# Two heads on the array at once, as row halves for the scores and column halves for the values, with interleaved selection chains and a hand-written TensorE order

## The chip, the cores and the metric

The kernel runs on one core of a Trainium2 chip. The metric is the device time of one execution in microseconds. The core has a matrix engine (TensorE, PE in the profile, with its weight loads as PEld), a vector engine (VectorE, DVE), an activation engine (ScalarE, ACT), GpSimd (POOL) and a queue that issues loads (SyncE, SP). [...]

## The reference

Attention that keeps, in each row, the 32 largest scores, followed by a mixer. All numbers are float32; the mixer's parameters arrive as float64.

```python
# q, k, v: (8 batches, 8 heads, 576 rows, 64)
scores = q @ k.T / sqrt(64)
kth = the 32nd largest score of each row
scores = where(scores >= kth, scores, -1e9)
attn = exp(scores - max)
attn = attn / (sum(attn) + 1e-9)
x = concat over heads of attn @ v          # (8, 576, 512)
# mixer, for each batch: U (576, 32), V (32, 576), w_ch1 (512, 2048), w_ch2 (2048, 512)
u = x + (x.T @ U @ V).T
out = u + maximum(u @ w_ch1, 0) @ w_ch2
```

## The kernel before

Heads go in pairs, four pairs to a batch, 32 in all. `prep` transposes q and k of a pair, so that head 0 has its 64 features on partitions 0 to 63 and head 1 on 64 to 127. The 576 query rows of a head are four chunks of 128 and a tail of 64; the two tails of a pair share one chunk. So a pair has nine score chunks (`CH`), a batch 36, the kernel 288.

For each chunk, `front` does the scores (line 198: two products of 64 features by 288 keys into two banks of PSUM, and ScalarE's copy to `Ssb` on line 205) and then the selection on VectorE. `select` finds the eight largest (`max`, line 215), replaces them by a very small number (`match_replace`, line 222, two instructions in the trace: a short load of the eight values and the replacement), and so on: four times `max`, three times `match_replace`, each on the result of the one before. ScalarE writes exp(score - max) into `E` meanwhile (lines 218 and 219), and line 224 sets to zero what is below the 32nd value.

Four chunks of a head make a `back_head`: `transposed` turns `E` on TensorE so that the keys are on the partitions (line 247; five key chunks, the last of 64 rows; ScalarE copies each to `PT`, line 249), and `values` multiplies: the turned probabilities (128 keys by 128 queries) are the stationary operand, v with a column of ones (65 columns) is streamed (line 255). The 65th column gives the row's sum, and `normalise` divides by it on VectorE (lines 265 to 267) and writes `X`. `back_tail` does the same for the tail chunk.

The mixer of a batch is a generator that yields shares of TensorE's work: U and V (lines 307 and 321), the turning of X (line 334), the first layer (line 345, with ScalarE's relu on line 355) and the second (line 362). `fill` takes pieces of the mixer of the batch before between the score chunks of the present one. The mixer of the last batch runs after all attention. The loop visits the chunks in order; what follows from a chunk comes two chunks later (`LAG`). The framework's planner then orders the instructions of each engine.

In the first 36 chunk steps the mixer's parameters are read and rounded to float32 on VectorE and GpSimd (`f64_round`), one parameter slab a step (`next_param`). SP's queue issues the loads of q, k, v and of the parameters, GpSimd's queue the stores of the output.

PSUM's eight banks: two for the scores (one buffer of two banks), two for transposes, one for `O`, three for the mixer.

Of the kernel before, what the change touches and what calls it, by code (L numbers as in the profile page):

```python
# [15 lines left out]
#: The upper word of 2**-126 as float64, read as float32: smaller magnitudes become 0.  # L16
# [4 lines left out]
def kernel(  # L21
# [33 lines left out]
    NV = 3  # L55

# [12 lines left out]
    vas = [const.tile([P, 2, NT + 1, D + 1], F32, name=f"va{i}") for i in range(NV)]  # L69
    for t in vas:  # L70
        nc.gpsimd.memset(t[:, :, :, D : D + 1], 1.0)
# [12 lines left out]
    def f64_raw(src):  # L84
# [16 lines left out]
        # Sign and top exponent bit stay; of the other ten exponent bits the lower seven.  # L101
# [43 lines left out]
    raw, qkTs, Xs = {}, {}, {}  # L145
    probs = {}

    def load(g):
# [14 lines left out]
        for i in range(2):  # L163
            nc.sync.dma_start(
                va[:, i, 0:NT, 0:D],
                v[b, h0 + i, 0:MAIN, :].rearrange("(p t) d -> p t d", t=NT),
            )
        nc.sync.dma_start(
            va[0:TAIL, :, NT, 0:D], v[b, h0 : h0 + 2, MAIN:S, :].rearrange("h p d -> p h d")
# [3 lines left out]
    def prep(g):  # L173
        """q and k of a pair of heads, transposed: [head and feature, (q | k), row]."""
        tiles = raw.pop(g)
        qkT = attn.tile([P, 2, S], F32, tag="qkT", name="qkT")
        for i, t in enumerate(tiles):
# [12 lines left out]
        qkTs[g] = qkT  # L190

    def scores(g, h, t, Ssb, r0):
        n = rows(t)
        hp = slice(h * D, (h + 1) * D)
        qkT = qkTs[g]
        sc = ps_s.tile([P, 2, 512], F32, tag="sc", name="sc")
        for i in range(2):
            nc.tensor.matmul(  # L198
                sc[0:n, i, 0:HALF],
                lhsT=qkT[hp, 0, cols(t)],  # L200
                rhs=qkT[hp, 1, i * HALF : (i + 1) * HALF],
                start=True,
                stop=True,
            )
        nc.scalar.copy(  # L205
            Ssb[r0 : r0 + n, :].rearrange("p (a n) -> p a n", a=2), sc[0:n, :, 0:HALF]
        )

    def select(Ssb):
        """exp(score - max) where the score is among the row's top TOPK, else 0."""  # L210
        E = attn.tile([P, S], F32, tag="E", name="E", bufs=8)
        cur = Ssb
        for i in range(TOPK // 8):
            m = small.tile([P, 8], F32, tag="m8", name="m8")
            nc.vector.max(m, cur)  # L215
            if i == 0:
                nmax = small.tile([P, 1], F32, tag="nmax", name="nmax", bufs=4)
                nc.scalar.mul(nmax, m[:, 0:1], -SCALE)  # L218
                nc.scalar.activation(E, Ssb, AF.Exp, bias=nmax, scale=SCALE)  # L219
            if i < TOPK // 8 - 1:  # L220
                nxt = attn.tile([P, S], F32, tag="rr", name="rr")
                nc.vector.match_replace(nxt, m, cur, NEG)  # L222
                cur = nxt
        nc.vector.scalar_tensor_tensor(  # L224
            out=E, in0=Ssb, scalar=m[:, 7:8], in1=E, op0=ALU.is_ge, op1=ALU.mult
        )
        return E

    def front(g, i):
        Ssb = attn.tile([P, S], F32, tag="Ssb", name="Ssb", bufs=3)  # L230
        if i < 2 * NT:
            scores(g, i // NT, i % NT, Ssb, 0)
        else:
            for h in range(2):
                scores(g, h, NT, Ssb, h * TAIL)
            del qkTs[g]
        probs[g, i] = select(Ssb)

    def transposed(chunks):
        """The chunks' probabilities with the keys on the partitions, a tile for each key chunk."""  # L240
        width = P * len(chunks)
        PTs = []
        for j in range(NT + 1):
            n = rows(j)
            tp = ps_t.tile([P, 4 * P], F32, tag="tp", name="tp")
            for i, E in enumerate(chunks):
                nc.tensor.transpose(tp[0:n, i * P : (i + 1) * P], E[:, cols(j)], ident)  # L247
            PT = attn.tile([P, 4 * P], F32, tag="PT", name="PT", bufs=6)
            nc.scalar.copy(PT[0:n, 0:width], tp[0:n, 0:width])  # L249
            PTs.append(PT)  # L250
        return PTs

    def values(O, PTs, va, h, c0, n):
        for j in range(NT + 1):
            nc.tensor.matmul(  # L255
                O,
                lhsT=PTs[j][0 : rows(j), c0 : c0 + n],
                rhs=va[0 : rows(j), h, j, :],
                start=(j == 0),
                stop=(j == NT),  # L260
            )

    def normalise(dst, O, n, m):
        den = small.tile([P, NT], F32, tag="den", name="den", bufs=4)
        nc.vector.tensor_scalar_add(den[0:n, 0:m], O[:, :, D], 1e-9)  # L265
        nc.vector.reciprocal(den[0:n, 0:m], den[0:n, 0:m])
        nc.vector.tensor_tensor(  # L267
            dst,
            O[:, :, 0:D],
            den[0:n, 0:m].rearrange("p m -> p m ()").to_broadcast([n, m, D]),  # L270
            ALU.mult,
        )
# [6 lines left out]
    def back_head(g, h):  # L279
# [172 lines left out]
```

## Time and profile before

| what | value |
|---|---|
| time, median of 3 runs | 2581.9 us (2578.86 to 2586.32) |
| span of the profiled execution | 2562.4 us (its own time isn't listed) |
| TensorE busy | 2431.2 us, 95% |
| TensorE's weight loads busy | 1503.1 us, 59% |
| VectorE busy | 1927.5 us, 75% |
| ScalarE busy | 848.4 us, 33% |
| mean granted TensorE clock | 0.888 |

The span runs from the first to the last instruction of the program; the time of a run also holds what lies around it. Matmuls are pipelined, so a busy TensorE isn't one at its peak, and an instruction's recorded duration is longer than the distance to the next one's start. Each fp32 product appears as two matmul instructions with a weight load each; a transpose as one.

### The profile page before, as it was taken

Reading aid. Unit: us, or ns where it says so; the run is one execution under the profiler, and the core shown is the slowest. Engines: PE = TensorE matmul, PEld = TensorE weight load, DVE = VectorE, ACT = ScalarE, POOL = GpSimd, SP = SyncE. Lnnn points to the kernel's source line nnn. Section 1 sums busy time; section 2 is a strip of 40 time slices with the busy share of each in tenths; the row PEclk is TensorE's granted clock in tenths of the full one; section 3 lists DMA queues with packets and bytes.
Section 4 is the critical chain, followed back from the end, with each engine's and each line's share of the span. In section 5 each row is a group of like instructions: output and inputs, shape, how many; then the busy total and the mean of one; then the engine's idle time right before and its main releaser. Section 6 shows DMA issues by size and latency. Waiting matters only on the chain.

```text
span 2562.4 us, 26533 instructions
## 1 busy us (share of the span) xinstructions
PE 2431.2 (95%) x9888; PEld 1503.1 (59%) x9888; DVE 1927.5 (75%) x3716; ACT 848.4 (33%) x1777; POOL 170.1 (7%) x157
## 2 busy tenths in 40 slices
PE   5586599999999999999999999999999999999998
PEld 3354366575656656575565656566565755666555
DVE  7999988877887787778777777877787787778300
ACT  2222233333333333333333334333342433334101
POOL 3445500000000000000000000000000000000000
PEclk9656589998899989999899989999899998999899
DMA  3222200000000000000000000000000000000000
GB/s 90 62 71 75 64 14 5 25 14 23 10 19 21 9 18 15 23 12 23 15 11 19 15 23 12 20 17 16 12 15 23 17 18 14 9 7 5 5 8 11
DMA packets 123202, 56.55 MB, mean 22 GB/s; under 512 B 116480, under 2 KB 116640, under 8 KB 123072
## 3 DMA queue, kind: packets, MB, share of 16 engines
q1 hardware_dynamic: 120128, 45.40, 7.0%
q0 software_dynamic: 2944, 9.44, 1.1%
q8 instruction: 78, 1.28, 0.2%
q14 instruction: 52, 0.43, 0.1%
HBM read 45.38 MB, written 9.44 MB: 21 GB/s over the span
## 4 chain that ended last, share of the span: by engine, by line
PE 89%; DVE 8%; issue 1%; ACT 1%; SPq 0%; DMA 0%; POOL 0%; DVEq 0%; ACTq 0%
PE mm L362 24%; PE mm L345 22%; PE O L255 16%; PE sc L198 14%; PE tp L247 7%; DVE m L215 3%; DVE rr L222 2%; PE mm L307 2%; PE mm L321 2%; PE tp L180 1%; PE tp L334 1%; DVE E L224 1%; DVE bits L105 1%; DVE bits L108 1%; DVE bits L102 0%
## 5 line engine op out<-in xcount | busy, mean ns | idle before, releaser
L215 DVE MAX8 m<-rr 128x8 f32<-128x576 f32 x864 | 654.6, 758 | 19.7
L362 PE MATMUL mm<-w,hT 128*128 128x512 f32 (+1 forms) x1280 | 633.7, 642 | 0.0
L345 PE MATMUL mm<-uT,w 128*128 128x256 f32 (+1 forms) x2048 | 578.0, 435 | 0.7 <-ACT uT L337 0.7
L198 PE MATMUL sc<-qkT 64*128 64x288 f32 (+1 forms) x1280 | 467.5, 479 | 11.8 <-ACT Ssb L205 11.3
L345 PEld LDWEIGHTS mm<-uT,w 128*128 128x128 f32 x2048 | 401.5, 203 | 131.6 <-issue 34.0
L255 PE MATMUL O<-va,PT 128*128 128x65 f32 (+3 forms) x3200 | 468.6, 287 | 0.5 <-DVE X L267 0.4
L255 PEld LDWEIGHTS O<-va,PT 128*128 128x128 f32 (+3 forms) x3200 | 415.3, 195 | 64.1 <-issue 10.4
L222 DVE MATCH_REPLACE8 rr<-m,rr 128x576 f32<-128x576 f32 x576 | 427.1, 741 | 0.0
L362 PEld LDWEIGHTS mm<-w,hT 128*128 128x128 f32 (+1 forms) x1280 | 233.4, 192 | 314.7 <-issue 309.9
L205 ACT COPY Ssb<-sc 128x576 f32<-128x576 f32 (+1 forms) x320 | 203.6, 636 | 511.4 <-PE sc L198 490.8
L215 DVE MAX8 m<-Ssb 128x8 f32<-128x576 f32 x288 | 216.0, 750 | 185.1 <-ACT Ssb L205 183.2
L198 PEld LDWEIGHTS sc<-qkT 64*128 64x128 f32 (+1 forms) x1280 | 215.4, 194 | 213.7 <-issue 108.1
L247 PE MATMUL tp<-ident,E 128*128 128x128 f32 (+1 forms) x1440 | 240.8, 298 | 105.0 <-DVE E L224 104.4
L247 PEld LDWEIGHTS tp<-ident,E 128*128 128x128 f32 (+1 forms) x1440 | 166.5, 143 | 210.0 <-DVE E L224 122.0
L249 ACT COPY PT<-tp 128x512 f32<-128x512 f32 (+3 forms) x480 | 212.0, 480 | 221.8 <-PE tp L247 221.4
L224 DVE SCALAR_TENSOR_TENSOR E<-Ssb,m,E 128x576 f32<-128x576 f32 x288 | 235.7, 818 | 12.1 <-ACT hT L355 0.5
L355 ACT ACTIVATE hT<-mm 128x320 f32<-128x320 f32 (+1 forms) x256 | 104.8, 409 | 421.4 <-PE mm L345 421.2
L219 ACT ACTIVATE E<-Ssb,nmax 128x576 f32<-128x576 f32 x288 | 223.4, 776 | 9.1
L222 DVE MATCH_REPLACE8 rr<-m,Ssb 128x576 f32<-128x576 f32 x288 | 213.6, 742 | 0.0
L218 ACT ACTIVATE nmax<-m 128x1 f32<-128x1 f32 x288 | 58.4, 203 | 367.9 <-DVE m L215 351.2
L265 DVE TENSOR_SCALAR den<-O 128x4 f32<-128x4 f32 (+1 forms) x96 | 14.7, 154 | 204.8 <-PE O L255 204.7
L374 POOL DMA_DIRECT2D out_dram<-ob x32 | 17.7, 555 | 1983.2 <-DVE ob L372 1983.2
(43 smaller groups left out, 786.4 us busy)
## 6 DMA issues: line engine op xcount, KB each, us to landing
raw<-in_moe_w_ch_dram SPq DMA_DIRECT2D x32, 512.0 KB, 3.7
ld_q<-in_q_dram SPq DMA_DIRECT2D x64, 128.0 KB, 2.7
ld_k<-in_k_dram SPq DMA_DIRECT2D x64, 128.0 KB, 2.7
va<-in_v_dram SPq DMA_DIRECT2D x64, 128.0 KB, 2.5
out_dram<-ob POOLq DMA_DIRECT2D x32, 256.0 KB, 2.5
ld_q<-in_q_dram SPq DMA_DIRECT2D x32, 32.0 KB, 2.4
ld_k<-in_k_dram SPq DMA_DIRECT2D x32, 32.0 KB, 2.4
va<-in_v_dram SPq DMA_DIRECT2D x32, 32.0 KB, 2.4
```

What stands on the lines that cost most here:

```text
L198: nc.tensor.matmul(sc[0:n, i, 0:HALF], lhsT=qkT[hp, 0, cols(t)], rhs=qkT[hp, 1, i * HALF : (i + 1) * HALF], start=True, stop=True,)
L205: nc.scalar.copy(Ssb[r0 : r0 + n, :].rearrange("p (a n) -> p a n", a=2), sc[0:n, :, 0:HALF])
L215: nc.vector.max(m, cur)
L219: nc.scalar.activation(E, Ssb, AF.Exp, bias=nmax, scale=SCALE)
L222: nc.vector.match_replace(nxt, m, cur, NEG)
L224: nc.vector.scalar_tensor_tensor(out=E, in0=Ssb, scalar=m[:, 7:8], in1=E, op0=ALU.is_ge, op1=ALU.mult)
L247: nc.tensor.transpose(tp[0:n, i * P : (i + 1) * P], E[:, cols(j)], ident)
L249: nc.scalar.copy(PT[0:n, 0:width], tp[0:n, 0:width])
L255: nc.tensor.matmul(O, lhsT=PTs[j][0 : rows(j), c0 : c0 + n], rhs=va[0 : rows(j), h, j, :], start=(j == 0), stop=(j == NT),)
L345: nc.tensor.matmul(ph[:, 0:width], lhsT=w1[:, cc, f * P : (f + 1) * P], rhs=uT[:, cc, 0:width], start=(cc == 0), stop=(cc == NC - 1),)
L355: nc.scalar.activation(hTs[f][:, 0:width], ph[:, 0:width], AF.Relu)
L362: nc.tensor.matmul(po[0:n, :], lhsT=hTs[f][:, offs[t] : offs[t] + n], rhs=w2[:, f, :], start=(f == 0), stop=(f == NF - 1),)
```

## The change

- A step is now one query chunk of both heads of a pair: five steps to a pair (the fifth is the two tails), 160 steps in all.
- Scores: for each half of the keys, head 0 (rows 0 to 63 of the array) and head 1 (rows 64 to 127) follow each other, into different banks. `ps_s` has two buffers, four banks.
- Selection: the two heads' chains take turns, instruction by instruction. Line 224's successor also writes the row's sum (`accum_out`), and v loses its column of ones.
- Values: v (keys by 64) is the stationary operand, and the turned probabilities (128 queries) are streamed. Head 0 writes partitions 0 to 63 of `O`, head 1 partitions 64 to 127, in turn. The result has the features on the partitions; ScalarE collects it in `XT`, and `to_x` turns it back on TensorE and multiplies by the reciprocal sums on VectorE. The tail's probabilities are divided on GpSimd before they are turned.
- Order: TensorE's instructions stay in the order of the program (`manual_schedule`); the planner orders the other engines. What follows from a step comes one step later. A step calls `fill` eight times, each with an eighth of the step's share of the mixer's two layers; the U and V part and the first turning of X go one piece to a call before that.
- The mixer's banks go from three to two, `O` uses the banks of the transposes. Two parameter slabs are read a step.

```diff
-    ps_s = ctx.enter_context(tc.tile_pool(name="ps_s", bufs=1, space=bass.MemoryType.PSUM))
+    ps_s = ctx.enter_context(tc.tile_pool(name="ps_s", bufs=2, space=bass.MemoryType.PSUM))
     ps_t = ctx.enter_context(tc.tile_pool(name="ps_t", bufs=2, space=bass.MemoryType.PSUM))
-    ps_o = ctx.enter_context(tc.tile_pool(name="ps_o", bufs=1, space=bass.MemoryType.PSUM))
-    ps_m = ctx.enter_context(tc.tile_pool(name="ps_m", bufs=3, space=bass.MemoryType.PSUM))
+    ps_m = ctx.enter_context(tc.tile_pool(name="ps_m", bufs=2, space=bass.MemoryType.PSUM))
+    ctx.enter_context(tc.manual_schedule(engines={PE}))
...
+    def scores(g, t):
+        qkT = qkTs[g]
+        n = rows(t)
+        S2 = attn.tile([P, 2, S], F32, tag="Ssb", name="Ssb", bufs=2)
+        scs = [ps_s.tile([P, 2, 512], F32, tag="sc", name="sc") for _ in range(2)]
+        for i, sc in enumerate(scs):
+            for h in range(2):
+                nc.tensor.matmul(
+                    sc[slice(0, n) if t < NT else half(h), h, 0:HALF],
+                    lhsT=qkT[half(h), 0, cols(t)],
+                    rhs=qkT[half(h), 1, i * HALF : (i + 1) * HALF],
+                    start=True,
+                    stop=True,
+                )
+        for i, sc in enumerate(scs):
+            cs = slice(i * HALF, (i + 1) * HALF)
+            if t < NT:
+                nc.scalar.copy(S2[:, :, cs], sc[:, :, 0:HALF])
...
+    def select(chunks, sums):
+        Es = [attn.tile([P, S], F32, tag="E", name="E", bufs=6) for _ in chunks]
+        curs, ms = list(chunks), [None] * len(chunks)
+        for i in range(TOPK // 8):
+            for c in range(len(chunks)):
+                m = small.tile([P, 8], F32, tag="m8", name="m8")
+                nc.vector.max(m, curs[c])
+                ms[c] = m
+                if i == 0:
+                    nmax = small.tile([P, 1], F32, tag="nmax", name="nmax", bufs=4)
+                    nc.scalar.mul(nmax, m[:, 0:1], -SCALE)
+                    nc.scalar.activation(Es[c], chunks[c], AF.Exp, bias=nmax, scale=SCALE)
+            if i < TOPK // 8 - 1:
+                for c in range(len(chunks)):
+                    nxt = attn.tile([P, S], F32, tag="rr", name="rr", bufs=4)
+                    nc.vector.match_replace(nxt, ms[c], curs[c], NEG)
+                    curs[c] = nxt
+        for c in range(len(chunks)):
+            nc.vector.scalar_tensor_tensor(
+                out=Es[c], in0=chunks[c], scalar=ms[c][:, 7:8], in1=Es[c],
+                op0=ALU.is_ge, op1=ALU.mult, accum_out=sums[c],
             )
...
+            den = small.tile([P, 1], F32, tag="dent", name="dent", bufs=2)
+            (E,) = select(chunks, [den])
+            nc.vector.tensor_scalar_add(den, den, 1e-9)
+            nc.vector.reciprocal(den, den)
+            nc.gpsimd.tensor_scalar(E, E, den, None, ALU.mult)
...
+    def back(g, t):
+        Es, va = probs.pop((g, t)), vas[g % NV]
+        nh = len(Es)
+        PT = attn.tile([P, NT + 1, 2, P], F32, tag="PT", name="PT")
+        per = 4 // nh
+        for j0 in range(0, NT + 1, per):
+            js = range(j0, min(j0 + per, NT + 1))
+            n = rows(js[0])
+            tp = ps_t.tile([P, per, nh, P], F32, tag="tp", name="tp")
+            for j in js:
+                for h, E in enumerate(Es):
+                    nc.tensor.transpose(tp[0 : rows(j), j - j0, h, :], E[:, cols(j)], ident)
+            nc.scalar.copy(PT[0:n, j0 : js[-1] + 1, 0:nh, :], tp[0:n, 0 : len(js)])
+            yield
+        m = rows(t)
+        O = ps_t.tile([P, P], F32, tag="tp", name="O")
+        for j in range(NT + 1):
+            for h in range(2):
+                nc.tensor.matmul(
+                    O[half(h), 0:m],
+                    lhsT=va[0 : rows(j), h, j, :],
+                    rhs=PT[0 : rows(j), j, h, :] if nh == 2 else PT[0 : rows(j), j, 0, half(h)],
+                    start=(j == 0),
+                    stop=(j == NT),
+                )
+        if t == 0:
+            XTs[g] = attn.tile([P, S], F32, tag="XT", name="XT")
+        nc.scalar.copy(XTs[g][:, cols(t)], O[:, 0:m])
+        yield
+
+    def to_x(g):
+        X, XT, den = get_x(g // NPAIR), XTs.pop(g), dens.pop(g)
+        cs = slice((g % NPAIR) * P, (g % NPAIR + 1) * P)
+        nc.vector.tensor_scalar_add(den, den, 1e-9)
+        nc.vector.reciprocal(den, den)
+        tp = ps_t.tile([P, NT, P], F32, tag="tp", name="tp")
         for t in range(NT):
+            nc.tensor.transpose(tp[:, t, :], XT[:, cols(t)], ident)
+        nc.vector.tensor_tensor(
+            X[:, 0:NT, cs].rearrange("p t (h d) -> p t h d", h=2),
+            tp.rearrange("p t (h d) -> p t h d", h=2),
+            den.rearrange("p t h -> p t h ()").to_broadcast([P, NT, 2, D]),
+            ALU.mult,
         )
+        yield
+        tp = ps_t.tile([P, P], F32, tag="tp", name="tp")
+        nc.tensor.transpose(tp[0:TAIL, :], XT[:, cols(NT)], ident)
+        nc.scalar.copy(X[0:TAIL, NT, cs], tp[0:TAIL, :])
+        yield
...
+    MLP_WORK = NF * NC * S / C + NF * (NT + 1) + 1.2
+    CH = NT + 1
+    STEPS = NP * CH
+    PARTS = 8
+    share = MLP_WORK / (NPAIR * CH * PARTS)
...
+    for n in range(STEPS + 1):
+        g, t = divmod(n, CH)
+        gb, tb = divmod(n - 1, CH)
         if g < NP:
+            if t == 0 and g + 1 < NP:
                 load(g + 1)
+            if t == 1:
+                ready = prep(g + 1) if g + 1 < NP else iter(())
+            front(g, t)
         next_param()
+        next_param()
+        fill(3)
+        if n >= 1:
+            for _ in back(gb, tb):
+                fill()
+            if tb == NT:
+                for _ in to_x(gb):
                     pass
+                if (gb + 1) % NPAIR == 0:
+                    mixing = mixed(gb // NPAIR)
+        if g < NP and t >= 1:
+            next(ready, None)
+        fill()
+    for _ in mixing:
         pass
+    for f in fillers:
+        for _ in f:
+            pass
```

## Rows read from the trace of the kernel before

**Rows 1.** Page, busy time of each engine, share and instructions.
```profile
PE 2431.2 (95%) x9888; PEld 1503.1 (59%) x9888; DVE 1927.5 (75%) x3716; ACT 848.4 (33%) x1777; POOL 170.1 (7%) x157
```

**Rows 2.** Windows: from:to, length, busy of PE, PEld, DVE, ACT, POOL; clock; DMA.
```profile
200.00:300.00 100.00, 65.88 (x275) 43.17 (x274) 99.93 (x200) 30.74 (x63) 52.91 (x36) 0.62 0.25 74
...
919.20:1216.20 297.00, 296.50 (x1239) 183.65 (x1237) 231.05 (x443) 105.95 (x222) 2.73 (x5) 0.92 0.07 17
...
1072.10:1075.60 3.50, 3.50 (x6) 1.00 (x6) 3.34 (x9) 0.00 (x0) 0.00 (x0) 0.51 0.00 0
```

**Rows 3.** Timeline of VectorE: start, duration, instruction; last line 224 of batches 0, 7.
```profile
323.25 0.80 DVE L224 SCALAR_TENSOR_TENSOR E<-Ssb,m,E 128x576 f32<-128x576 f32 x1
...
2394.79 0.82 DVE L224 SCALAR_TENSOR_TENSOR E<-Ssb,m,E 128x576 f32<-128x576 f32 x1
```

**Rows 4.** Timeline of TensorE, merged: start, duration, instructions and their count.
```profile
1014.16 3.60 PE L362 MATMUL mm<-w,hT 128*128 128x512 f32 x8
1017.68 1.23 PE L198 MATMUL sc<-qkT 64*128 64x288 f32 x4
1018.85 3.70 PE L362 MATMUL mm<-w,hT 128*128 128x512 f32 x8
1022.48 1.23 PE L198 MATMUL sc<-qkT 64*128 64x288 f32 x4
...
1028.15 0.75 PE L198 MATMUL sc<-qkT 64*128 64x288 f32 x2
1028.83 1.09 PE L247 MATMUL tp<-ident,E 128*128 128x128 f32 x8
```

**Rows 5.** Groups of the period 919.2 to 1216.2: busy, mean ns, idle before.
```profile
L255 PE MATMUL O<-va,PT 128*128 128x65 f32 (+3 forms) x403 | 57.9, 283 | 0.0
L198 PE MATMUL sc<-qkT 64*128 64x288 f32 (+1 forms) x160 | 53.9, 448 | 0.5 <-ACT Ssb L205 0.5
```

**Rows 6.** Timeline of TensorE's matmuls and weight loads in one block of values.
```profile
1066.12 0.62 PE L247 MATMUL tp<-ident,E 128*64 128x128 f32 x4
1066.59 0.56 PE L255 MATMUL O<-va,PT 128*128 128x65 f32 x4
...
1067.66 4.52 PE L255 MATMUL O<-va,PT 64*128 64x65 f32 x32
1072.12 1.11 PE L362 MATMUL mm<-w,hT 128*64 128x512 f32 x1
...
1067.42 4.62 PEld L255 LDWEIGHTS O<-va,PT 64*128 64x128 f32 x32
```

**Rows 7.** Timeline of VectorE inside a period.
```profile
1205.73 0.76 DVE L215 MAX8 m<-rr 128x8 f32<-128x576 f32 x1
...
1207.38 0.76 DVE L215 MAX8 m<-rr 128x8 f32<-128x576 f32 x1
1208.06 0.74 DVE L215 MAX8 m<-Ssb 128x8 f32<-128x576 f32 x1
1208.72 0.80 DVE L224 SCALAR_TENSOR_TENSOR E<-Ssb,m,E 128x576 f32<-128x576 f32 x1
1209.43 0.08 DVE L222 MATCH_VALUE_LOAD rr<-m,Ssb 128x8 f32 x1
1209.51 0.74 DVE L222 MATCH_REPLACE8 rr<-m,Ssb 128x576 f32<-128x576 f32 x1
1210.17 0.68 DVE L372 TENSOR_TENSOR ob<-X,mm 128x512 f32<-128x512 f32 x1
```

**Rows 8.** Groups over the whole span, by shape: a GpSimd product with a scalar.
```profile
L115 POOL TENSOR_SCALAR mask<-mask 128x512 f32<-128x512 f32 x32 | 47.6, 1487 | 13.9 <-DVE mask L113 13.9
```

**Rows 9.** Timeline of TensorE near the end, with what ended its wait.
```profile
2395.59 0.66 PE L247 MATMUL tp<-ident,E 128*128 128x128 f32 x4 [0.24 <-ACT PT L249]
```

**Rows 10.** Waits in the period 919.2 to 1216.2: total us, times, longest.
```profile
DVE m L215 <- ACT Ssb L205: 26.5, 15, 4.0
DVE den L265 <- PE O L255: 26.5, 9, 6.4
```

More of the change, by code (lines that the diff above doesn't have):

```diff
@@ L81, in cols, with half @@
         return slice(t * P, t * P + rows(t))
+    def half(h):
+        return slice(h * D, (h + 1) * D)
     def f64_raw(src):
@@ L209, in select @@
[L209 to L227, printed above, removed]
@@ L253, in values @@
[L253 to L272, printed above, removed]
+        S2 = attn.tile([P, 2, S], F32, tag="Ssb", name="Ssb", bufs=2)
@@ new lines, in scores @@
+        return [S2[:, 0], S2[:, 1]] if t < NT else [S2[:, 0]]
+    def select(chunks, sums):
[17 more added lines that the diff above has]
+            nc.vector.scalar_tensor_tensor(
+                out=Es[c],
+                in0=chunks[c],
+                scalar=ms[c][:, 7:8],
+                in1=Es[c],
+                op0=ALU.is_ge,
+                op1=ALU.mult,
+                accum_out=sums[c],
+            )
+        return Es
@@ new lines, in front @@
+    def front(g, t):
+        if t == 0:
+            dens[g] = small.tile([P, NT, 2], F32, tag="den", name="den", bufs=3)
+        chunks = scores(g, t)
+        if t < NT:
+            probs[g, t] = select(chunks, [dens[g][:, t, h : h + 1] for h in range(2)])
+        else:
+            den = small.tile([P, 1], F32, tag="dent", name="dent", bufs=2)
[3 more added lines that the diff above has]
+            nc.gpsimd.tensor_scalar(E, E, den, None, ALU.mult)
+            probs[g, t] = [E]
+            del qkTs[g]
@@ L315, in mixer @@
         nc.scalar.copy(Tb, pT[0:R, :])
-        yield 5
-        for t in range(NT + 1):
+        yield
+        for t in (0, 1, NT, 2, 3):
             n = rows(t)
@@ L356, in mixer @@
                 yield NC * width / C
-            for t in chunks:
+            for i, t in enumerate(chunks):
                 n = rows(t)
@@ L376, in mixer @@
                     nc.gpsimd.dma_start(out[b, MAIN:S, :], ob[0:n, :])
-                yield 4
-    MIXER_WORK = 5 + (NT + 1) + 0.3 * (NT + 1) + NF * NC * S / C + NF * (NT + 1)
-    CH = 2 * NT + 1
-    LAG = 2
-    per_step = MIXER_WORK / (NPAIR * CH - 1)
-    filler, due = iter(()), 0.0
-    def fill(work):
-        nonlocal due
-        due += work
-        while due > 0:
-            done = next(filler, None)
-            if done is None:
-                due = 0.0
-                break
-            due -= done
+                yield 2
@@ new lines, in mlp, with fill @@
+                if k == 0 and i < 2:
+                    if i == 0:
+                        ahead = turn(b, HALVES[1])
+                    turned = next(ahead)
+                    yield 0.6
+        del Xs[b]
+    MLP_WORK = NF * NC * S / C + NF * (NT + 1) + 1.2
[3 more added lines that the diff above has]
+    share = MLP_WORK / (NPAIR * CH * PARTS)
+    fillers, mixing, due = [], iter(()), 0.0
+    def fill(n=1):
+        nonlocal due
+        for _ in range(n):
+            next(mixing, None)
+            due += share
+            while due > 0:
+                if not fillers:
+                    due = 0.0
+                    break
+                done = next(fillers[0], None)
+                if done is None:
+                    fillers.pop(0)
+                else:
+                    due -= done
@@ L397, with mixed @@
+    def mixed(b):
+        yield
+        yield from mix(b)
+        for first in turn(b, HALVES[0]):
+            yield
+        fillers.append(mlp(b, first))
     load(0)
     next_param()
-    prep(0)
-    for n in range(NP * CH + LAG):
-        g, i = divmod(n, CH)
+    for _ in prep(0):
+        pass
+    for n in range(STEPS + 1):
+        g, t = divmod(n, CH)
+        gb, tb = divmod(n - 1, CH)
         if g < NP:
-            if i == 0 and g + 1 < NP:
+            if t == 0 and g + 1 < NP:
@@ L404 @@
                 load(g + 1)
-            front(g, i)
-            if i == CH - 2 and g + 1 < NP:
-                prep(g + 1)
+            if t == 1:
+                ready = prep(g + 1) if g + 1 < NP else iter(())
+            front(g, t)
         next_param()
-        fill(per_step)
-        gb, ib = divmod(n - LAG, CH)
-        if n >= LAG and ib in (NT - 1, 2 * NT - 1):
-            back_head(gb, ib // NT)
-        elif n >= LAG and ib == CH - 1:
-            back_tail(gb)
-            if (gb + 1) % NPAIR == 0:
-                for _ in filler:
-                    pass
-                filler, due = mixer(gb // NPAIR), 0.0
```

115 lines of the change are left out of this document (38 added, 77 removed).

## Prediction

> **What bounds the kernel now.** I read the totals of the page first, then the stretches, one period in its groups, and last the order of time inside it. The page has TensorE busy nearly throughout and VectorE three quarters of the time [rows 1]; that is a mean over three stages. Up to 324 us, batch 0's attention, VectorE bounds: in its third hundred it is busy for 99.9 us and TensorE for 65.9 [rows 2]. From there to 2395.6 us attention of one batch runs beside the mixer of the one before; the two rows of the last line 224 of batch 0 and of batch 7 stand 2071.5 us apart, seven periods of 296 us [rows 3]. In one such period (297 us) TensorE is busy for 296.5, VectorE for 231 at a granted clock of 0.92 [rows 2]: TensorE bounds, and VectorE's idle time follows from it. After 2395.6 us TensorE is alone for 167 us. So:
>
> span = 324 + 7 x 296 + 167 = 2563 (2562.4 on the page).
>
> The three runs have a median of 2581.9, which is 19.5 over the profiled span; the time of the profiled execution itself isn't listed, so I add 19.5 at the end. The runs spread by 0.29%, so 0.3% is about what a measurement can tell from no change.
>
> **Scores on TensorE.** Every fp32 product is two instructions in the trace. A visit of two of line 198 takes 28.83 - 28.15 = 0.68 us, one of four takes 18.85 - 17.68 = 1.17 [rows 4]: 0.245 each (0.85 ns a column), and 0.19 that doesn't depend on their number. The eight of line 362 behind a visit take 3.63 us, those behind other 128-row work 3.52 [rows 4]: 0.11 more to get back. A visit to 64-row operands thus costs 0.30 beside its streaming. Before, two chunks make two or more visits; the period spends 53.9 us in 160 such instructions [rows 5]. After, one visit a step has eight instructions: i=0 for head 0 (two), head 1 (two), then i=1 for both. No row shows two halves at work at once. Bounds: one after another, 8 x 0.245 + 0.30 = 2.26 us; overlapped, where the second instruction of a product runs beside the first of the other head's, 5 slots, 1.22 + 0.30 = 1.52. Twenty steps: 45.2 or 30.4, a gain of 8.7 or 23.5. I take the second: the two heads' operands stand in different partitions, go to different banks and depend on nothing of each other.
>
> **Values.** Before, 128 columns of probabilities are loaded as weights to stream 65 columns: 32 in 72.12 - 67.66 = 4.46 us, 0.139 each with the 64-row chunk's visits in it, though 65 columns stream in 0.055 [rows 6]. They are bound by the loads. The period spends 57.9 us in them [rows 5]. After, v (64 columns) is loaded and 128 queries stream: 20 instructions a step at 0.109. One after another 2.18 + 0.30 = 2.48; overlapped, 11 slots, 1.20 + 0.30 = 1.50. A tail streams 64 columns: 20 x 0.054 + 0.30 = 1.38. Sixteen steps and four tails: 45.2 or 29.5, a gain of 12.7 or 28.4; I take the second for the same reason.
>
> On the loads the rows say that they hide: 32 loads with 128 rows fill 4.62 us beside the 32 matmuls [rows 6]. [...]
>
> **Added on TensorE.** XT goes back through 20 transposes a period at 0.12 (eight in 1.09) [rows 4]: 2.4 us. E's transposes and the mixer's instructions keep their number; q's and k's are only spread over three steps.
>
> **Clock.** [...] The drop at 1072.1 us comes at the end of the 4.5 us block of 65-column values [rows 2, 6]. Such blocks disappear: each step's transposes and values are cut by pieces of the mixer. Bounds: nothing back, or all 8%. I take half: 0.96.
>
> TensorE's period: 297 - 23.5 - 28.4 + 2.4 = 247.5, times 0.92/0.96 = 237.
>
> **VectorE.** Dependent, MAX8 to MAX8 over a replacement takes 1.65 us; on to an independent MAX8 or line 224 it is 0.68 and 0.66, line 224 to the next 0.71, value load 0.08, replacement to something independent 0.66 [rows 7]. With two chains interleaved a chunk takes 4 x 0.68 + 3 x 0.74 + 0.71 = 5.65 us, where a lone one takes about 6.3. Period: 36 x 5.65 = 203; the lone tail chains 4 x 3 x 0.23 = 2.8; sixteen small sums and reciprocals, taken as two value loads each, 2.6; the scaled X, four at 0.68, and the mixer's ten sums at 0.68 [rows 7], 9.5. The row sums that line 224 now writes: from nothing to one more pass of 0.71; I take 0.1, as it is one value a row, nearest to the value load's 0.08: 3.6. Total 222.
>
> [...]
>
> **New waits.** TensorE's order is now the program's: scores of step n, three shares of mixer, then the transposes of step n-1, which wait for line 224 of that step; behind them stand all of the mixer and the next scores. VectorE has the scores of step n before, so it doesn't stand still meanwhile; its full step (11.3 + 0.2 + 0.35) is close to TensorE's, its tails are half as long, so it can catch up there. Between the three groups of transposes and the values there is a share each, but a share is smaller than a piece, so some are empty, and then TensorE waits for the copy, as the 0.24 us on line 249 before [rows 9]; twice a step, 10 us at most. Two mixer banks in place of three can wait for ScalarE's relu behind an exp. The tail's division moves to GpSimd, 1.5 us for a nearby shape [rows 8]; three shares of mixer lie before its reader. I put 13 us for all of these. Period: 250.
>
> **Start and end.** Batch 0: VectorE is full already [rows 2], as the parameters' rounding fills the gaps of the chains, so the interleaving finds little to fill; two parameters a step are the rate of one a chunk. DMAs keep number and size, but for a 64-wide v and three memsets gone. I leave 324. At the end a tail is left in place of a head and a tail, but one step of the mixer of batch 6 is still due: 167 stays.
>
> Sum: 324 + 7 x 250 + 167 = 2241, + 19.5 = 2260.
>
> **Rivals.**
> 1. The halves don't run at once, or one kind doesn't. Both: 297 - 8.7 - 12.7 + 2.4 = 278 and 5 of waits, 283 a period: 2491. One kind: 263 and 5, 2387. For it: nothing in the trace shows overlap. Against: independence as above. 0.14.
> 2. VectorE becomes the bound. It waits 26.5 us a period for ScalarE's score copies and 26.5 for TensorE's values before reading them [rows 10], harmless today. If as much stays, by sums placed early in its queue, 222 + 53 = 275 a period: 2435. A second pass of line 224 for its row sums is 36 x 0.71 = 25 more, 247, some 260 with waits, and 25 at the start: 2356. Both 0.10. [...]
> 3. The loads of column halves don't hide: 20 x (0.054 + 0.109) + 0.30 = 3.56 a step, 20 x 0.109 + 0.30 = 2.48 a tail, 67 us in place of 29.5, 287 a period: 2520. The trace speaks against it. 0.03. [...]
> 4. Slower: a change of half empties the array, as going to 64 rows and back does, 0.15 each way. Each step changes half about 13 times: 260 x 0.15 = 39 on top of rival 1's 283, 322 a period: 2765. It decides from 0.05 us a change, where the period is 296 again. For it: 128-row and 64-row operands do cost this. Against: four transposes with 64-column weights between 128-column ones take 66.59 - 66.12 = 0.47 us, without a visible gap [rows 6]. 0.08.
> 5. Gains and waits cancel, 0.03. And better: no waits at all, 237 or less: under 2170, 0.06.
>
> The forecast keeps 0.56. The range goes from 2170 (237 a period) to 2500, just over rival 1; outside lie rivals 3 to 5, 0.20. The likeliest case alone: 2190 to 2345 (240 to 262 a period). Faster 0.89, within 0.3% 0.03, slower 0.08.
>
> **What would show it.** Scores: a step's eight instructions of 288 columns start to the next work in 1.5 us, not 2.3. Values: twenty in 1.5, not 2.5, with starts closer than 0.109. Clock: 0.96 or more between 324 and 2070 us, fewer low stretches. VectorE: MAX8 to MAX8 0.68; line 224 to its successor 0.8; 222 us busy in a period. Waits: TensorE idle about 13 a period, on line 224's successor and on PT's copy. The prediction fails if products of the two halves start 0.109 or 0.245 apart, if TensorE waits over 2 us a step for the selection, or if the clock falls below 0.9.

## The result, and the profile after

The changed kernel takes 2250.2 us (median of four runs, 2249.9 to 2251.6), the kernel before 2580.4 beside it; the ratio is 0.873 [0.8704, 0.8756]. 2260 was predicted. The profiled execution took 2251.6 us, 1.8 more than its span.

The windows below cut the span at the end of the last line 245 (line 224's successor) of batch 0, 328.8, and of batch 7, 2059.9 (the first and the last row of VectorE's timeline further down, as [rows 3] of before); the columns are those of [rows 2], the clock a share of full speed.

```profile
0.00:328.80 328.80, 144.13 (x788) 92.18 (x788) 318.10 (x629) 95.85 (x214) 162.62 (x117) 0.60 0.24 70
328.80:2059.90 1731.10, 1626.91 (x8681) 946.68 (x8682) 1494.78 (x3234) 751.01 (x1742) 67.25 (x61) 0.96 0.07 18
2059.90:2249.80 189.90, 182.52 (x581) 102.51 (x579) 9.26 (x17) 19.15 (x46) 5.61 (x8) 0.98 0.03 9
...
566.90:815.00 248.10, 233.52 (x1247) 135.79 (x1248) 213.67 (x463) 108.00 (x250) 9.73 (x9) 0.96 0.08 20
...
580.00:589.80 9.80, 5.71 (x12) 1.22 (x12) 9.80 (x21) 2.42 (x5) 0.00 (x0) 1.00 0.00 0
589.80:610.20 20.40, 16.29 (x24) 5.95 (x25) 5.24 (x10) 1.17 (x2) 0.00 (x0) 0.50 0.00 1
610.20:815.00 204.80, 200.06 (x1150) 122.77 (x1150) 186.48 (x405) 98.99 (x231) 7.46 (x7) 1.00 0.08 21
```

The span is 328.8 + 7 x 247.3 + 189.9. One period has TensorE busy for 233.5 of 248.1 us; it is idle for 14.6. The last three rows cut this one period from 580.0 on, and there the mean falls apart: for 205 us the clock is 1.00 and TensorE idle for 4.7 us; the rest of the idle time and all of the low clock lie in the first 43 us, the border between two batches.

TensorE's groups of that period (busy, mean ns, idle before) and its waits (total, times, longest):

```profile
L295 PE MATMUL O<-PT,va 128*64 128x128 f32 (+3 forms) x400 | 27.1, 272 | 1.3 <-ACT PT L289 1.2
L209 PE MATMUL sc<-qkT 64*128 64x288 f32 (+1 forms) x160 | 24.6, 426 | 0.0
```

```profile
PE mm L349 <- DVE X L350: 6.9, 3, 5.3
PE mm L336 <- DVE X L316: 2.3, 1, 2.3
PE tp L288 <- ACT PT L289: 1.5, 4, 0.6
PE tp L288 <- DVE E L245: 1.2, 4, 0.4
PE O L295 <- ACT PT L289: 1.2, 2, 0.7
```

Scores (line 209) stood at 53.9 us and values (line 295) at 57.9 [rows 5]. The first two waits are the mixer's and sit at the border: its first product waits for X, and its V products (line 349) for the addition of the result into X on VectorE (line 350). The waits that the prediction named, for the copy of PT and for line 245, are 3.9 us of 14.6.

TensorE's timeline, first the border, then two ordinary steps, and last a stretch of the end:

```profile
577.12 1.24 PE L209 MATMUL sc<-qkT 64*128 64x288 f32 x8
580.64 4.59 PE L336 MATMUL mm<-X,U 128*32 128x512 f32 x10 [2.28 <-DVE X L316]
...
592.36 2.07 PE L349 MATMUL mm<-Tb,V 32*128 32x512 f32 x2 [5.33 <-DVE X L350]
594.35 3.78 PE L399 MATMUL mm<-w,hT 128*128 128x512 f32 x4
...
618.31 1.24 PE L209 MATMUL sc<-qkT 64*128 64x288 f32 x8
...
646.70 1.46 PE L295 MATMUL O<-PT,va 128*64 128x128 f32 x20
648.09 2.42 PE L382 MATMUL mm<-uT,w 128*128 128x320 f32 x8
650.44 1.24 PE L209 MATMUL sc<-qkT 64*128 64x288 f32 x8
651.61 2.42 PE L382 MATMUL mm<-uT,w 128*128 128x320 f32 x8
...
656.66 0.95 PE L295 MATMUL O<-PT,va 128*64 128x64 f32 x20
657.54 0.66 PE L315 MATMUL tp<-ident,XT 128*128 128x128 f32 x4
...
2083.37 28.42 PE L399 MATMUL mm<-w,hT 128*128 128x512 f32 x64
2111.64 8.78 PE L382 MATMUL mm<-uT,w 128*128 128x320 f32 x32
```

A visit of eight score instructions takes 651.61 - 650.44 = 1.17 us, as long as one of four before [rows 4]. A full step of values takes 648.09 - 646.70 = 1.39, a tail 0.88. At the border 41 us lie between one step's scores and the next (577.12 and 618.31). VectorE in that time, between the two rows that mark the batches:

```profile
328.00 0.82 DVE L245 SCALAR_TENSOR_TENSOR E<-Ssb,m,E 128x576 f32<-128x576 f32 x1
...
590.88 0.81 DVE L245 SCALAR_TENSOR_TENSOR E<-Ssb,m,E 128x576 f32<-128x576 f32 x1
591.62 0.08 DVE L245 DVE_READ_ACCUMULATOR E<-Ssb,m,E 128x1 f32 x1
591.62 0.68 DVE L350 TENSOR_TENSOR X<-X,mm 128x512 f32<-128x512 f32 x1
...
620.32 1.42 DVE L233 MAX8 m<-Ssb 128x8 f32<-128x576 f32 x2 [1.22 <-ACT Ssb L219]
...
631.45 1.42 DVE L233 MAX8 m<-Ssb 128x8 f32<-128x576 f32 x2
...
2059.09 0.82 DVE L245 SCALAR_TENSOR_TENSOR E<-Ssb,m,E 128x576 f32<-128x576 f32 x1
```

The first addition stands behind the selection that ends at 591.62; then VectorE has nothing to select until 620.32, as the next scores are behind the V products in TensorE's order. An ordinary step of two interleaved chains takes 631.45 - 620.32 = 11.13 us, 5.57 a chunk.

### The profile page after: what moved, and what is told of

Same layout as the page of the kernel before. It is cut to its first block, busy times and chain, and to the rows that moved or that the text cites. A ratio compares the mean times of both kernels' runs of the same rounds, so it can differ in the third digit from the quotient of the medians.

```text
span 2249.8 us, 27480 instructions
## 1 busy us (share of the span) xinstructions
PE 1953.6 (87%) x10048; PEld 1141.4 (51%) x10048; DVE 1822.1 (81%) x3876; ACT 866.0 (38%) x2001; POOL 235.5 (10%) x186
## 4 chain that ended last, share of the span: by engine, by line
DVE 46%; PE 36%; issue 13%; ACT 4%; DMA 0%; POOL 0%; SPq 0%; POOLq 0%; DVEq 0%; ACTq 0%
DVE m L233 19%; DVE rr L242 17%; PE mm L399 13%; PE mm L382 8%; PE O L295 5%; DVE E L245 4%; PE sc L209 4%; PE tp L288 3%; PE mm L349 2%; ACT Ssb L219 2%; DVE bits L114 1%; ACT E L238 1%; ACT PT L289 1%; DVE bits L111 1%; DVE X L316 1%
## 5 line engine op out<-in xcount | busy, mean ns | idle before, releaser
L233 DVE MAX8 m<-rr 128x8 f32<-128x576 f32 x864 | 614.1, 747 | 1.9
L382 PE MATMUL mm<-uT,w 128*128 128x256 f32 (+1 forms) x2048 | 545.4, 412 | 1.5 <-ACT hT L392 1.4
L382 PEld LDWEIGHTS mm<-uT,w 128*128 128x128 f32 x2048 | 372.5, 190 | 123.4 <-issue 32.9
L289 ACT COPY PT<-tp 128x512 f32<-128x512 f32 (+1 forms) x448 | 209.5, 495 | 320.0 <-PE tp L288 319.1
L295 PE MATMUL O<-PT,va 128*64 128x128 f32 (+3 forms) x3200 | 236.8, 288 | 19.7 <-ACT PT L289 18.9
L295 PEld LDWEIGHTS O<-PT,va 128*64 128x64 f32 (+1 forms) x3200 | 173.0, 146 | 113.4 <-issue 60.1
L209 PE MATMUL sc<-qkT 64*128 64x288 f32 (+1 forms) x1280 | 210.3, 450 | 0.3 <-ACT qkT L188 0.3
L219 ACT COPY Ssb<-sc 128x576 f32<-128x576 f32 x256 | 152.3, 640 | 117.9 <-PE sc L209 115.3
L209 PEld LDWEIGHTS sc<-qkT 64*128 64x128 f32 (+1 forms) x1280 | 110.0, 187 | 89.7 <-issue 66.2
L267 POOL TENSOR_SCALAR E<-E,dent 128x576 f32<-128x576 f32 x32 | 56.7, 1772 | 802.3 <-DVE dent L266 755.0
```

What stands on the lines that cost most here:

```text
L209: nc.tensor.matmul(sc[slice(0, n) if t < NT else half(h), h, 0:HALF], lhsT=qkT[half(h), 0, cols(t)], rhs=qkT[half(h), 1, i * HALF : (i + 1 ...
L219: nc.scalar.copy(S2[:, :, cs], sc[:, :, 0:HALF])
L233: nc.vector.max(m, curs[c])
L289: nc.scalar.copy(PT[0:n, j0 : js[-1] + 1, 0:nh, :], tp[0:n, 0 : len(js)])
L295: nc.tensor.matmul(O[half(h), 0:m], lhsT=va[0 : rows(j), h, j, :], rhs=PT[0 : rows(j), j, h, :] if nh == 2 else PT[0 : rows(j), j, 0, half ...
L382: nc.tensor.matmul(ph[:, 0:width], lhsT=w1[:, cc, f * P : (f + 1) * P], rhs=uT[:, cc, 0:width], start=(cc == 0), stop=(cc == NC - 1),)
```

## The experiments

Ratios are to the kernel before, timed beside each. "Period" is a seventh of the distance between the last line 245 of batch 0 and of batch 7, as above. The kernel before took 2572.5 to 2583.9 us beside these runs, so a few us between two of them say nothing.

**Scores head by head**, the four instructions of head 0 and then those of head 1.

```diff
-        for i, sc in enumerate(scs):
-            for h in range(2):
+        for h in range(2):
+            for i, sc in enumerate(scs):
```

> The eight score products' instructions of a step are issued head 0 first, then head 1, so that two halves of the array meet only once in a visit. Theory (the row halves run at once, and TensorE bounds the period outside the batch's border): the visit grows from 1.17 us to 1.9 (seven slots of 0.245 and 0.2) or 2.15 (none shared), 15 to 20 us a period, 105 to 140 in all: 2340 to 2390. Rival (VectorE bounds after the change, as the chain of waits has 46% on it): TensorE's extra time hides, below 2290.

2268.8 us, 0.8788 [0.8755, 0.8821], the period 249.7. That is below 2290, as the rival said, but not for its reason: the visit is unchanged, so TensorE has no additional time that could hide. The theory's longer visit is wrong. The instructions that run in its first 0.04 us, and in the next 0.13 (windows of line 209 alone):

```profile
656.33:656.37 0.04, 0.03 (x2) 0.03 (x2) 1.00 0.00 0
656.37:656.50 0.13, 0.13 (x2) 0.13 (x4) 1.00 0.00 0
```

Two start together. The trace doesn't name the head, but two instructions of one head don't (four of them take as long as this visit of eight, as the next run shows); so one is the first and the other the fifth in the order, and the halves overlap in either order. What costs 18 us is probably the copy, whose two halves now both need late products: ScalarE's wait for the scores goes from 115.3 to 175.8 us over the span. That wasn't tried by itself.

**Scores with a piece of the mixer between the heads.** `piece` takes the next piece of the mixer's two layers and subtracts it from what is due.

```diff
-        for i, sc in enumerate(scs):
-            for h in range(2):
+        for h in range(2):
+            if h:
+                piece()
+            for i, sc in enumerate(scs):
```

> A piece of the mixer's work stands between head 0's two pairs of score instructions and head 1's, so that the two row halves never run together. Theory (the gain of the scores is the overlap of the two halves): a visit of 1.17 us becomes two of about 1.1 each, 20 times a period, so TensorE's work grows by 20 to 25 a period and the time by 120 to 170, to 2370 to 2420. Rival 1 (the gain was the fewer visits alone, and overlap gives nothing): under 2290. Rival 2 (TensorE's growth is hidden under VectorE's selection): under 2290 with TensorE's busy time up by over 100.

2414.9 us, 0.937 [0.9342, 0.9397], the period 270.4. That is 23.1 a period more for 20 additional visits, 1.16 each (the trace has 1.17 for a visit of four instructions). One visit of eight with no overlap would be 8 x 0.245 + 0.19 = 2.15; so 0.98 of the 1.16 is the overlap, and 0.19 the second visit. TensorE's busy time in the seven periods grows by 166 us (1626.9 to 1792.9) and the time by 165: nothing is hidden, and both rivals fall.

**Values head by head.**

```diff
-        for j in range(NT + 1):
-            for h in range(2):
+        for h in range(2):
+            for j in range(NT + 1):
```

> The twenty value instructions of a step are issued head 0 first, then head 1; same weights, same streams, and VectorE's order is the same. Theory (the column halves run at once): starts go from 0.054 us apart to about 0.107, a full step from 1.39 to 2.2 to 2.4 us, 14 to 18 us a period: 2335 to 2370. Rival A (the gain of the values is only that 64 columns are loaded in place of 128): no change, 2245 to 2260. Rival B (VectorE bounds): below 2290, though the starts spread.

2388.1 us, 0.9251 [0.9217, 0.9285], the period 266.3. Windows of one full step, cut at the 64-row chunk of each head:

```profile
693.22:694.20 0.98, 0.97 (x8) 1.00 0.00 0
694.20:694.60 0.40, 0.40 (x4) 1.00 0.00 0
...
```

The same two stretches follow for head 1. Nothing overlaps: 2.76 us a step in place of 1.39, where the theory had 2.2 to 2.4, and so the time is 18 us above its range. Unlike the scores, the order decides here; or it is the 64-row chunk between the heads, so:

**The same with the 64-row chunks last.**

```diff
-        for j in range(NT + 1):
-            for h in range(2):
+        for h, js in ((0, range(NT)), (1, range(NT)), (0, (NT,)), (1, (NT,))):
+            for j in js:
```

> The values head by head for the four chunks of 128 rows, and then the 64-row chunk of both heads: eight instructions of one column half stand in a row, with no change of the row count between the heads. Theory (column halves run together only where instructions of the two stand next to each other): no overlap, a full step of 2.3 to 2.8 us in place of 1.39, a period 18 to 25 us longer, and 2340 to 2390. Rival (the halves ran apart in the run by heads because of the visit to the 64-row chunk between them, and one half's instructions can pass the other's, as the scores' did): a full step of 1.4 to 1.6 and 2245 to 2280.

2289.6 us, 0.8879 [0.8863, 0.8895], the period 252.4, outside both ranges. A step takes 1.88 us:

```profile
652.78:653.26 0.48, 0.48 (x4) 1.00 0.00 0
...
653.24:653.26 0.02, 0.02 (x2) 1.00 0.00 0
653.26:653.28 0.02, 0.02 (x4) 1.00 0.00 0
...
653.27:653.62 0.35, 0.35 (x9) 1.00 0.00 0
```

(An instruction that lies across a cut counts on both sides.) Head 0's first four of eight run alone. At 653.26 us two of them are still running, and two more start within 0.02 us of each other. As starts of one half stand 0.109 apart (a step of the changed kernel has two starts, one of each half, at 646.86 us, two more at 646.97 and two at 647.08), these must be head 0's fifth and head 1's first. From there starts come twice as densely, until head 0 is through. Both expectations are partly right: column halves did pass each other, but only over the last four, and with a change of row count between them (the run before), not at all.

**Selection chains one after the other.** The loops `for c in range(len(chunks))` become one outside the loop over `i`, and line 245's instruction ends it.

```diff
-        for i in range(TOPK // 8):
-            for c in range(len(chunks)):
+        for c in range(len(chunks)):
+            for i in range(TOPK // 8):
...
```

> Both heads' selections are written one after the other in place of turn by turn. VectorE's chunk goes from about 5.6 us to 6.3, 22 us a period. Theory (TensorE bounds, VectorE is 95% busy outside the batch's border): it overtakes TensorE by 8 to 13 us a period there: 2310 to 2345. Rival A (VectorE bounds): all 22, and as much at the start: about 2420. Rival B (only TensorE counts): below 2270.

2356.7 us, 0.9129 [0.9095, 0.9162], the period 263.0: above the theory's range and below rival A. TensorE's waits for the selection in the seven periods, first in the changed kernel and then here (lines are three less):

```profile
PE tp L288 <- DVE E L245: 7.4, 24, 0.7
...
PE tp L285 <- DVE E L242: 131.8, 79, 3.9
```

VectorE is busy for 15.0 us a period more (1494.8 to 1599.5 in seven), and the period grows by 15.7: none of it hides. Rival A has the periods nearly right and the start wrong, which gets 7 us shorter (321.4). The interleaving is worth 106 us with the rest of the change in place: VectorE stands so close behind TensorE that a longer chain shows.

**TensorE's order by the planner.** Only the line for the hand order is left out.

```diff
-    ctx.enter_context(tc.manual_schedule(engines={PE}))
```

> The framework's planner orders TensorE's instructions again; nothing else differs. Theory (the gain is the halves' overlap, the order by hand adds little): 2190 to 2290; if the planner moves scores ahead of the products with V at the batch's border, below 2250. Rival (the order by hand carries the gain, because it keeps the halves' instructions next to each other and VectorE fed): above 2400.

2161.6 us, 0.8375 [0.8338, 0.8411], the fastest: 89 us under the changed kernel. The period is 234.3. The seven periods together, one of them, its first 50 us, and two stretches of another one's border:

```profile
329.10:1969.10 1640.00, 1607.02 (x8684) 938.49 (x8681) 1493.77 (x3233) 750.83 (x1742) 67.24 (x61) 0.98 0.07 19
...
795.40:1027.00 231.60, 227.58 (x1250) 133.84 (x1249) 213.61 (x462) 107.40 (x249) 9.72 (x9) 1.00 0.08 21
...
795.00:845.00 50.00, 49.37 (x226) 24.27 (x225) 39.92 (x85) 18.72 (x40) 2.57 (x3) 1.00 0.04 12
...
579.40:589.20 9.80, 9.80 (x24) 3.37 (x22) 8.45 (x17) 0.78 (x2) 0.54 (x1) 1.00 0.07 28
589.20:599.50 10.30, 10.30 (x42) 6.36 (x42) 2.67 (x5) 3.77 (x8) 0.00 (x0) 0.50 0.00 0
```

The idle border is gone: TensorE is idle for 33 us in the seven periods, where it was for 104. That is 71 of the 91 us by which they got shorter; the other 20 are busy time, at a clock of 0.98 in place of 0.96. In the period from 795.4 the clock stays at 1.00. In five of the seven it still falls for a while, and not for want of work: from 589.2 it is 0.50 after 9.8 us in which TensorE was busy throughout, with the mixer's products, those with V among them. TensorE's timeline in the period from 795.4 shows what the planner did (lines are one less):

```profile
816.64 4.56 PE L398 MATMUL mm<-w,hT 128*128 128x512 f32 x10
821.13 0.76 PE L208 MATMUL sc<-qkT 64*128 64x288 f32 x4
821.82 1.12 PE L348 MATMUL mm<-Tb,V 32*128 32x512 f32 x2
```

Ten instructions of the mixer's second layer and half of the next scores stand between two V products.

The next runs keep the hand order and ask what at the border costs it.

**Five calls of filler after each V product**, and the share sized for the calls that there are.

```diff
-            if t % 2:
+            for _ in range(5):
                 yield
...
-    share = MLP_WORK / (NPAIR * CH * PARTS)
+    share = MLP_WORK / (NPAIR * (CH * PARTS - 1))
```

> Five filler steps instead of one or none now lie between the V products of the mixer in TensorE's order by hand, and the filler's share is sized for the steps that call it. Theory (the border between batches loses TensorE time because the V products stand in front of the next scores and of the mixer's other products, and each waits for an add queued on VectorE): TensorE's 14.6 us of idle time a period fall below 5 and the clock of the border rises from 0.80 towards 1.00; the period falls from 247 to 232 to 236, and with the left-over filler at the end gone (20 to 25) the time is 2110 to 2190. Rival (the loss is the selection chain's own and merely shows at the border): the waits move to the products behind and the time is 2220 to 2260.

2297.5 us, 0.8911 [0.8885, 0.8938]: slower, outside both ranges. The period is 253.4. TensorE's idle time in the seven periods grows by 35 of their 43 us. In a period looked at, three of the five additions still stand behind a whole selection, and now the mixer's second layer also waits, for the addition into the output (line 409). The end doesn't get shorter either (193.2 us) despite the corrected share, as 25 calls in place of two now lie before the batch's two layers. What the share alone does in this order wasn't run. Waits of one period:

```profile
PE mm L399 <- DVE ob L409: 7.0, 1, 7.0
PE mm L349 <- DVE X L350: 5.1, 1, 5.1
```

**The additions first on VectorE.**

```diff
-            nc.vector.tensor_tensor(X[0:n, t, :], X[0:n, t, :], pu[0:n, :], ALU.add)
+            with tc.high_priority():
+                nc.vector.tensor_tensor(X[0:n, t, :], X[0:n, t, :], pu[0:n, :], ALU.add)
```

> The five adds into X of the mixer go ahead of the selection in VectorE's order; TensorE's order stays. Theory (the add is late because it is queued behind the selection of two heads): the waits of the V products for X, 32.0 us in all, fall below 10, and with the clock that they cost the time falls by 25 to 70, to 2180 to 2225. Rival (the next scores are what is late, since they stand behind the V products in TensorE's order, and the add costs little): the time falls by less than 15.

2223.8 us, 0.8632 [0.8601, 0.8663]; the V products' waits for X fall from 32.0 to 16.3 us, less than expected (below 10), the time by 26, as expected.

**The V products in the transposes' banks.**

```diff
-            pu = ps_m.tile([P, C], F32, tag="mm", name="mm")
+            pu = ps_t.tile([P, C], F32, tag="tp", name="tp")
```

> The V products write to the transposes' PSUM buffers instead of the two that they share with the mixer's accumulating product. Theory (two buffers, one of them held by the accumulating product, make each V product wait for the add before it): the waits of V products for X fall from 32.0 to below 12, and the time falls by 20 to 60. Rival (the V products then wait for the copies of the transposes, or the transposes behind them for the adds, and the wait only changes its name): 2240 to 2270.

2206.8 us, 0.8568 [0.8538, 0.8598], 43 us less; the wait falls to 11.9 us. One of the mixer's two banks is held by the second layer's accumulating product, so that V products had one left; that was the larger part of the wait. The seven periods got 46 us shorter: 23 of it is TensorE's idle time, and 23 its busy time, as the clock rose from 0.96 to 0.98.

**Both of these.**

```diff
-            pu = ps_m.tile([P, C], F32, tag="mm", name="mm")
+            pu = ps_t.tile([P, C], F32, tag="tp", name="tp")
...
+            with tc.high_priority():
```

> The hand order with both the adds ahead and the V products in the transposes' buffers. If the two take the same wait, 2195 to 2215, as the buffers alone (2206.8). If they take two waits, their gains of 26 and 43 add up: 2175 to 2190. What then lies above the planner's order (2161.6) is the cost of the next scores standing behind the V products.

2201.8 us, 0.8536 [0.8523, 0.855]: they took the same wait. V products now wait for additions for 0.5 us in all, yet 40 us remain to the planner's order. TensorE's idle time in the seven periods is 70 us here and 33 there, which is 37 of the 40. Its waits in them, first here and then in the planner's order:

```profile
PE mm L336 <- DVE X L316: 24.7, 7, 4.0
PE tp L288 <- ACT PT L289: 13.2, 20, 1.9
PE O L295 <- ACT PT L289: 12.6, 23, 0.8
...
PE tp L287 <- ACT PT L288: 4.7, 14, 0.7
PE O L294 <- ACT PT L288: 1.8, 6, 0.4
PE mm L335 <- DVE X L315: 1.3, 3, 0.6
```

The first product of the mixer waits for X once a batch, and transposes and values wait for ScalarE's copies of PT; the planner's order has little of either (it waits longest for the selection, 13.1 us). The expectation put the remainder down to the next scores, which stand behind the V products. VectorE does stand without scores for some 11 us at a border, but no wait of TensorE shows that this costs time. Neither of these waits was taken away by itself.

**The planner's order with the corrected share**, and then also with V products in the transposes' banks (the last two lines).

```diff
-    ctx.enter_context(tc.manual_schedule(engines={PE}))
...
-    share = MLP_WORK / (NPAIR * CH * PARTS)
+    share = MLP_WORK / (NPAIR * (CH * PARTS - 1))
...
-            pu = ps_m.tile([P, C], F32, tag="mm", name="mm")
+            pu = ps_t.tile([P, C], F32, tag="tp", name="tp")
```

> The planner's order with the filler's share sized for the seven calls that a tail step makes. Theory (28 calls of filler are left over and run at the end): the last 26 us of the batch before the last leave the end, which falls from 191 to 165 to 170, while the periods grow by 3 to 4 each: 2155 to 2170 if TensorE bounds the period, 2135 to 2145 if they don't grow. Rival (the work at the end is not the filler's left-over): the end stays at 191.

> The planner's order, the share as before it, and the V products in the transposes' buffers. Theory (the two mixer buffers still make V products and the mixer's other products wait in the planner's order): 10 to 30 below the run that only has the share. Rival (the planner already fills these waits): within 8 of it.

2163.5 us (0.8389 [0.8372, 0.8407]) and 2168.8 (0.8409 [0.8394, 0.8424]): neither gains. In the first the end does fall, from 191.0 to 161.9 us, and its second layer from 224 instructions to 184. The last batch's own layer is 160 of these, as the end before had. But the period grows from 234.3 to 239.3, 35 us in seven, more than the end gave back (in the profiled run, the slowest of its four); with the work that came in, the clock of the periods fell from 0.98 to 0.96. The second shows that the planner had already filled the waits for banks.

## Why the prediction was right

**TensorE bounds, and the work falls by half in scores and values: right.** Scores: 20 x 1.17 = 23.4 us a period, 25.6 with the 0.11 that the prediction counts for the work behind each visit, where 30.4 were forecast. The term was mis-sized by a slot: eight instructions of two halves take four times 0.245 and not five, and the 0.19 beside them. Values: 16 x 1.39 + 4 x 0.88 = 25.8 in place of 29.5. A full step takes ten slots of 0.109 beside the 0.30, and not eleven, and the tails overlap as well, which the forecast took one after another (1.38). That the halves run at once at all the prediction argued from their independence alone; the runs with the halves apart show it (1.16 us more for each visit of scores, 2.76 in place of 1.39 for a step of values), and rival 1 falls. The values' halves depended on the order: a step took 1.39 in turn, 1.88 and 2.76 head by head. The scores' visit took 1.17 and 1.18 in the two orders.

**Loads of column halves (rival 3): fallen.** Its 0.054 us for a load is an estimate, 64 columns at the 0.85 ns of a streamed one, and no run shows a load at that price. In the 1.39 us of a full step there are 20 loads, and the streaming alone, one after another, is 20 x 0.109 = 2.18 us. In pairs, one start of each half, the products start 0.109 apart (646.86, 646.97, 647.08); 128 columns at 0.85 ns are 0.109, so a pair's two loads add nothing. Rival 4, a price for each change of half, falls with it: at 0.15 the nine changes among the ten products of a step would be 1.35 us, which the 1.39 can't hold beside the streaming. The change to 64 rows does stop the step: after 647.52 no product and no load of it starts until 647.72.

**VectorE: the sum right, and little room.** 222 us a period were forecast and 213.7 measured. A chunk takes 5.57 us, 5.65 forecast. TensorE has the longer work, but in the run with the chains apart 15 us more a period on VectorE showed in full. Rival 2's periods of 275 or 260 us didn't come. The row sums cost at most 0.03 us a chunk, 0.1 forecast: the next instruction starts 0.74 us after line 245 (590.88 to 591.62), with the read of the accumulator in it, where line 224 took 0.71 [rows 7]. A second pass would have been 0.71. (The 247 that the prediction gives for such a pass counts 3.6 us twice: 222 - 3.6 + 25.6 is 244.)

**Waits: the size right, the place wrong.** 13 us were forecast for transposes that wait for copies and selections and for two mixer banks behind the relu; 14.6 were measured, 3.9 of it there. Nearly all of the rest is at the border, which the prediction costed at nothing: it had the V products among the mixer's pieces and didn't ask what stands behind them in a fixed order, nor that the accumulating product holds one of the two banks. With V products in other banks the time falls by 43 us, in the planner's order by 89; TensorE's idle time in the seven periods falls by 23 and by 71.

**Clock: the size right by luck.** 0.96 was forecast, as half of what there was to gain, and is granted. But what remains low isn't left of blocks of values: it is 20.4 us at 0.50 in the border, after 9.8 us in which TensorE was busy for 5.7. That idle time brings the clock down isn't shown: the planner's order has little of it at the border, and its clock still falls there in five periods of seven, 0.98 in the mean.

**Start, end and the offset.** 328.8 for 324. The end has 189.9 for 167: 64 more second-layer instructions of the batch before, 2111.64 - 2083.37 = 28.3 us, mostly because a tail's step calls the filler seven times where the share counts on eight: the corrected share, in the planner's order, took 40 of the 64 away. No run says why the other 24 stay. The 19.5 us added to the span turned out to be 1.8: the prediction took the difference between one profiled span and the median of other runs for work around the span, but runs of the kernel before lie up to 10 us below that median (2571.65).

The sum: 324 + 7 x 250 + 167 + 19.5 = 2260 against 328.8 + 7 x 247.3 + 189.9 + 1.8 = 2251.6 for the profiled run. The period was 19 us too long in seven and the offset 18; start and end were 28 too short. The forecast is nearer than its parts, and that is luck: errors of 37 one way and 28 the other.

**Of the parts that a run took out, one costs time:** the order by hand. Without it the other parts give a ratio of 0.8375. The prediction spoke of the hand order only through its waits inside a step and had no rival for it. With the rest in place, the overlap of the scores is worth 165 us, that of the values 138 and the interleaving 106.

## What to carry to other kernels

When an order is fixed by hand, look not at the ordinary step but at the place where a serial chain (product, addition, product) stands in front of the next independent work: here late additions on VectorE made TensorE wait for 32.0 us in the seven periods, and at one border VectorE had nothing to select for 28.7 us. With the V products in other banks the periods got back 23 us of idle time and 23 of busy time, at a clock of 0.98 in place of 0.96; in the planner's order the clock fell to 0.50 without any idle time. Packing two half-size operands paid where their instructions stood next to each other (eight score instructions in 1.17 us, as long as four of one head; column halves in turn, with the same row count, 1.39 us a step, and 2.76 head by head); check the visit's length against that of one operand alone. Before moving work from the end into the middle (one run here gained 29 us at the end and lost 35 in the periods), see that the middle has idle time to take it.

## What was not expected of the hardware

- Row halves started out of order: in the run by heads two instructions started within 0.04 us of each other, which must be the first and the fifth.
- Column halves of 128 rows passed each other only over four instructions when eight of one half stood in front, and not at all across a change to 64 rows. That change had a price: ten instructions at 0.109 are 1.09 us, and eight and the two of 64 rows took 0.98 + 0.40 = 1.38.
- Line 245, an accumulating VectorE instruction with two float32 sources of 128x576, cost at most 0.03 us more than line 224 without the accumulator (0.74 and 0.71), its read of 0.08 us included.
